# Spreading the value and sum matmuls of the first batch over the units, and reordering the second pair, in a hash-attention and maxout-FFN kernel

## The chip, the cores and the metric

The kernel runs on one core of a Trainium2 chip. Its engines work side by side and meet through semaphores: TensorE (PE, with weight loads listed as PEld), VectorE (DVE), ScalarE (ACT), GpSimd (POOL), and SyncE (SP), which here only issues DMAs. The metric is device time in microseconds of one execution; the time of the kernel before is the median of three.

## The reference

```python
def _attn_ref(q, k, v, proj):                      # q, k, v: 4 x 8 x 768 x 64, proj: 64 x 6
    scale = 1.0 / np.sqrt(D)
    q_bits = (np.einsum('bhsd,dk->bhsk', q, proj) > 0).astype(np.int64)
    k_bits = (np.einsum('bhsd,dk->bhsk', k, proj) > 0).astype(np.int64)
    q_bucket = np.sum(q_bits * powers, axis=-1)
    k_bucket = np.sum(k_bits * powers, axis=-1)
    mask = q_bucket[:, :, :, None] == k_bucket[:, :, None, :]
    scores = scale * np.matmul(q, k.transpose(0, 1, 3, 2))
    scores = np.where(mask, scores, -1000000000.0)
    ...                                            # softmax over keys
    return np.matmul(attn, v)

def _moe_ref(x, w1, w2, w3, w_out):                # x: 3072 x 512 from the heads, w1..w3: 512 x 768
    h = np.maximum(np.maximum(x @ w1, x @ w2), x @ w3)
    return h @ w_out                               # w_out: 768 x 512
```

Queries and keys of a head are hashed to six bits; a query attends only to keys in its bucket. The heads of a token, side by side, are the input of a three-way maxout layer and an output projection.

## The kernel before, in words

**Pairs and units.** Two heads make a pair; there are 16 pairs, four to a batch. A pair is computed in 12 units, six for each half of the queries (qh, 384 queries). One unit is one head (hd) and two of the six chunks of 128 keys (kp). So there are 192 units; a group is six units with the same pair and query half, and slot is the unit's number within it. For each unit `scores` (L299 on) does two matmuls of bf16 operands from the tile S into a two-bank PSUM tile sc (pool of two), and ACT takes the exponential into one of 14 fp16 tiles AT. S holds for each side (0 queries, 1 keys) and head 64 rows of data and six rows of bits (plus or minus 0.5), in an even and an odd half of the positions, so that a matmul over 70 rows gives the score with the bucket penalty.

**Preparation of a pair** (`prep_groups`). Four transpose groups (`tgroup`: three PE transposes into a PSUM tile mp, a DVE copy to the SBUF tile T2, and for pairs 2 to 7 a second DVE copy of the odd rows to S). The first of them runs `begin`, which also issues on POOL the q and k loads of the pair two further on. Then `hashes`: eight matmuls of T2 with the projection into bp, the comparison on DVE (bits, L208), and four DMAs that put bits into S (L214), on POOL's queue, though for pair 1 those of head 0 go by SP. Then `even`, one POOL cast (L217), and for pair 1 `odd`, two DVE casts (L221). `do_hash` calls the odd casts given as the last list, then the hash, and appends the rest to the list `late`, from which one entry is taken in each unit. For pair 1 that list is odd, odd, even.

**Values and sums.** With the exponentials of six units there, 24 matmuls of 32 columns give the values (av, one PSUM bank in a pool of its own) and 12 give partial sums (sm, from the pool ms_ps of three banks, which transposes, hashes and the FFN use too). DVE then empties them: sv (L350), avs (L351), ys (L353). In `values` they run one unit behind the group. From the second pair to unit 59 the value matmuls of the first four chunks run at slot 4 of the group itself (`EARLY_CH`). The sums pass through DMAs (dd, rd, rb) for the normalisation: gather, then `invert`, `spread` and `scale` at set numbers of units later; scale, on POOL, writes xT, the FFN's input (L388).

**The order** is written out by hand in one loop over the units (L415 on). In unit u it issues: loads of v and of weights due there, `scores(u + 1)`, normalisation steps that are due, one entry of `late`, then on some slots a transpose group or a hash (`fill`), the early values, FFN groups once the batch is complete (from unit 61 on), and after a group's end the values. Every engine executes its own instructions in this order. Ahead of the loop stand nine warming matmuls (L400) and the first pair's preparation. After unit 60 two query halves are evaluated together, and the change leaves that part alone.

**Unit order within a group.** For pair 0 the units are sorted by head (head 0's three units, then head 1's); for the others head alternates.

Of the kernel before, what the change touches and what calls it, by code (L numbers as in the profile page):

```python
# [9 lines left out]
FP32 = mybir.dt.float32  # L10
# [7 lines left out]
def kernel(  # L18
# [12 lines left out]
    nc = tc.nc  # L31
    B, H, S, D = q.shape
    NBITS = proj.shape[1]
    P = 128
    NCH = S // P

    HALF = S // 2
    CH2 = NCH // 2
# [17 lines left out]
    ODD_LATE, ODD_PSUM = 1, 8  # L56
# [18 lines left out]
    av_ps = ctx.enter_context(tc.tile_pool(name="av_ps", bufs=1, space=bass.MemoryType.PSUM))  # L75
    ms_ps = ctx.enter_context(tc.tile_pool(name="ms_ps", bufs=3, space=bass.MemoryType.PSUM))
# [9 lines left out]
    def load_proj():  # L86
        for par in range(2):
            rows = slice(par * D, (par + 1) * D)
            nc.scalar.dma_start(pst[rows, :], proj[:, :])
            nc.vector.tensor_copy(pj[rows, 1 + par, 0:NBITS], pst[rows, :])  # L90
            nc.vector.tensor_copy(pj[rows, 0, par : 2 * NBITS : 2], pst[rows, :])
# [3 lines left out]
    ones = konst.tile([P, 32], FP16, name="ones")  # L95
    nc.vector.memset(ones[:], 1.0)

    NAT = 14
    at_tiles = [konst.tile([P, 2, HALF + 2], FP16, name=f"AT{i}", tag=f"AT{i}") for i in range(NAT)]
# [7 lines left out]
    natural, trans, vones = {}, {}, {}  # L107
# [25 lines left out]
    def prep_groups(pi):  # L133
# [85 lines left out]
        def odd(side):  # L219
            copy = nc.scalar.copy if pi > ODD_LATE else nc.vector.tensor_copy  # L220
            return lambda: copy(st["S"][0:D, side, :, 1, :], st["T2"][D : 2 * D, side])  # L221
# [7 lines left out]
                    lambda: bits_first(1, early[2:]), lambda: bits_first(0, ((0, 1, 0, HALF),)),  # L229
                    lambda: bits_first(1, ((0, 1, 0, HALF),))]  # L230
        odds = [odd(1), odd(0)]
        if pi == ODD_LATE:
            return [tgroup(s, h) for h in (0, 1) for s in (1, 0)], hashes, odds + [even], []
        return [tgroup(s, h) for h in (0, 1) for s in (1, 0)], hashes, [even], odds if pi >= ODD_PSUM else []

    def ffn_groups(b):
        xb = xts[b]
# [44 lines left out]
    units = []  # L282
    for pi in range(NPAIR):
        for qh in range(2):
            inner = [(kp, hd) for kp in range(NCH // 2) for hd in range(2)]
            units += [(pi, qh, kp, hd) for kp, hd in (sorted(inner, key=lambda e: e[1]) if pi == 0 else inner)]
    unit_of = {e: u for u, e in enumerate(units)}
    NU = len(units)
    UPB = NU // B
    UPG = NCH  # L290
    UPP = 2 * UPG
    WEIGHTS_AT = (2, 4, 6, 8) + tuple(range(12, 48, 5)) + (63, 67, 71)
    FFN_AT = 13
    EARLY_CH = 4
    FIRST = 2
    PAIRS_AT = UPB + UPP
    xts, avs_of, ys_of = {}, {}, {}
# [18 lines left out]

    started = {}

    def values_part(pi, qh, c0, c1, own=True):
        if (pi, qh) not in started:  # L320
            started[pi, qh] = (av_ps if own else ms_ps).tile([P, 512], FP32, tag="av" if own else "ms", name="av")
        av = started[pi, qh]
        for c in range(c0, c1):
            for hd in range(2):
                at = at_tiles[unit_of[pi, qh, c // 2, hd] % NAT]
                for vh in range(2):
                    p0, d0 = hd * D + 32 * vh, c * D + 32 * vh
                    nc.tensor.matmul(av[p0 : p0 + 32, 0 : HALF + 1], vones[pi][:, hd, d0 : d0 + 32],  # L328
                                     at[:, c % 2, 0 : HALF + 1], start=(c == 0), stop=(c == NCH - 1))
        return av  # L330

    def values(pi, qhs, c0=0):
        at_of = lambda qh, hd, c: at_tiles[unit_of[pi, qh, c // 2, hd] % NAT]
        banks = []
        for qh in qhs:
            av = values_part(pi, qh, c0, NCH, qh == qhs[0])
            sm = ms_ps.tile([P, 512], FP32, tag="ms", name="sm")
            for s in range(CH2):
                for hd in range(2):
                    for half in range(2):  # L340
                        c, t = half * CH2 + s, 2 * hd + half
                        nc.tensor.matmul(sm[32 * t : 32 * t + 32, 0:HALF], ones[:, :],  # L342
                                         at_of(qh, hd, c)[:, c % 2, 0:HALF], start=(s == 0), stop=(s == CH2 - 1))
            banks.append((qh, av, sm))
        if pi not in avs_of:
            avs_of[pi] = avspool.tile([P, 2, HALF], FP32, tag="avs", name="avs")
            ys_of[pi] = yspool.tile([P, 2, HALF], FP32, tag="ys", name="ys")
        for qh, av, sm in banks:
            sv = small.tile([P, 1], FP32, tag="sv", name="sv")
            nc.vector.tensor_scalar(out=sv[:], in0=av[:, HALF : HALF + 1], scalar1=EPS, scalar2=None, op0=AluOp.mult)  # L350
            nc.vector.tensor_scalar(out=avs_of[pi][:, qh, :], in0=av[:, 0:HALF], scalar1=sv[:], scalar2=None,  # L351
                                    op0=AluOp.add)
            nc.vector.tensor_scalar(out=ys_of[pi][:, qh, :], in0=sm[:, 0:HALF], scalar1=EPS * S / 2, scalar2=None,  # L353
                                    op0=AluOp.add)
        if pi % HPAIR == HPAIR - 1:
            return normalize(pi, qhs[0], 1)
        return normalize(pi, 0, 2) if 1 in qhs else []
# [38 lines left out]

    with tc.manual_schedule():
        wm = ms_ps.tile([P, 512], FP32, tag="ms", name="wm")
        for _ in range(9):
            nc.tensor.matmul(wm[:], warm[:, 0:P], warm[:], start=True, stop=True)  # L400
        load(0, nc.sync)
        load_proj()
        load(1, nc.sync)
        cast_v = {0: load_v(0, nc.sync)}
        load(2, nc.sync)
        first = prep_groups(0)
        for g in first:
            g()

        prep, hash_ready, late, ffn, steps = [], [], [], [], []  # L410
        f_credit = 0.0
        for p2 in range(1, NPAIR):
            ts, *hs = prep_groups(p2)
            prep += [(p2, i, g, hs) for i, g in enumerate(ts)]
        for u in range(NU):  # L415
            pi = units[u][0]
            b, ub = divmod(u, UPB)
            if u % UPP == 0 and pi + 1 < NPAIR:
                cast_v[pi + 1] = load_v(pi + 1, nc.gpsimd)
            if u == FIRST:  # L420
                cast_v[0]()
            if u % UPP == 10 and pi + 1 < NPAIR:
                cast_v[pi + 1]()
            if u in WEIGHTS_AT:
                nc.gpsimd.dma_start(*weight_parts.pop(0))
            if ub == FFN_AT and b > 0:
                ffn += ffn_groups(b - 1)
            if FIRST < u + 1 < NU:
                scores(u + 1)
            for e in [e for e in steps if e[0] <= u]:  # L430
                e[1]()
                steps.remove(e)
            if late:
                late.pop(0)()
            slot = u % UPG
            if u <= UPG:
                fill = u >= FIRST
            else:
                fill = slot in (2, 3, 5) if u < UPB + FFN_AT else slot in (1, 4)
            if fill:  # L440
                if hash_ready and u < PAIRS_AT:
                    do_hash()
                elif prep and prep[0][0] < pi + AHEAD:
                    _, i, g, hs = prep.pop(0)
                    g()
                    if i == 3:
                        hash_ready.append(hs)
            if slot == 4 and UPP < u < PAIRS_AT:
                values_part(*units[u][0:2], 0, EARLY_CH)
            f_credit = min(f_credit + 0.66, 1.4)  # L450
            while ffn and f_credit > 0:
                c, g, _ = ffn.pop(0)
                g()
                f_credit -= c
            if u >= UPG - 1 + LAG and (u - LAG) % UPG == UPG - 1:
                vp, vq = units[u - LAG][0:2]
                single = vp * UPP < PAIRS_AT or vp % HPAIR == HPAIR - 1
                if single or vq == 1:
                    steps += [(u + n, g) for n, g in values(vp, (vq,) if single else (0, 1),
                                                            EARLY_CH if (vp, vq) in started else 0)]  # L460
                    if u >= PAIRS_AT and vq == 1:
                        do_hash()

        steps = [(n - NU, g) for n, g in steps]
        steps += values(NPAIR - 1, (1,))
        steps.sort(key=lambda e: e[0])
        at = 0
        for c, g, _ in ffn + ffn_groups(B - 1):
            while steps and steps[0][0] <= at:
                steps.pop(0)[1]()  # L470
            g()
            at += c
# [30 lines left out]
```

## Time and profile before

| what | value |
|---|---|
| median of three executions | 299.92 us (297.75 to 301.09) |
| profiled execution, its own time | 300.85 us |
| its span, first to last instruction | 299.1 us |
| mean granted TensorE clock | 0.988 |
| PE busy | 288.8 us (97%) |
| ACT busy | 194.6 us (65%) |
| DVE busy | 190.3 us (64%) |
| POOL busy | 139.8 us (47%) |
| DMA moved | 35.90 MB |

The span is shorter than the time by what lies around the first and last instruction. Busy times are of one execution, each engine by itself; they overlap. The slices of the page are 40 equal parts of the span, each about 7.5 us, with a digit for tenths of busy time. A unit of the first batch takes about 0.95 us (seven groups from 34.26 to 74.55 us); the FFN's first matmul starts at 75.21 us.

### The profile page before, as it was taken

The numbers are of one execution on the slowest core, as the hardware profiler recorded it, in microseconds if no ns is written. First come the engines' busy times: TensorE is split into PE (matmuls) and PEld (weight loads), VectorE is DVE, ScalarE is ACT, GpSimd is POOL, SyncE is SP. The second block draws the span as 40 slices with busy tenths as digits, with TensorE's granted clock in tenths as the row PEclk, the third lists the DMA queues.
The fourth block names the chain that finished last, engine by engine and source line by source line (L and its number), as shares of the span: only waits on it lengthen the run. The fifth ranks groups of instructions, "written<-read, shape, count | busy, mean of one in ns | idle before, by whom it ended". The sixth has DMA issues, their size and how long they took to land.

```text
span 299.1 us, 6790 instructions
## 1 busy us (share of the span) xinstructions
PE 288.8 (97%) x2593; PEld 162.6 (54%) x2593; DVE 190.3 (64%) x419; ACT 194.6 (65%) x238; POOL 139.8 (47%) x187
## 2 busy tenths in 40 slices
PE   8879999899999999999999999999999999999994
PEld 3444444444566556565566556665655555555551
DVE  2873688877877367663777467663766266758480
ACT  3764888988584966879586966879596957110202
POOL 2762769888874718184723808082700702220000
PEclk9995999999999999999999999999999999999999
DMA  7885088767593442618050452414111211230202
GB/s 211 263 196 154 13 235 184 152 191 212 138 256 104 147 142 66 209 33 278 20 161 30 124 177 59 109 33 160 33 56 37 96 51 46 80 132 2 105 0 106
DMA packets 20277, 35.90 MB, mean 120 GB/s; under 512 B 6081, under 2 KB 12485, under 8 KB 20245
## 3 DMA queue, kind: packets, MB, share of 16 engines
q0 software_dynamic: 8992, 19.81, 24.9%
q1 hardware_dynamic: 10948, 15.52, 16.7%
q8 instruction: 20, 0.33, 0.5%
q10 hardware_dynamic: 304, 0.13, 0.2%
q14 instruction: 13, 0.10, 0.1%
HBM read 31.46 MB, written 6.39 MB: 127 GB/s over the span
## 4 chain that ended last, share of the span: by engine, by line
PE 90%; DMA 3%; ACT 2%; POOL 2%; DVE 1%; issue 1%; SPq 0%; ACTq 0%; POOLq 0%
PE l L246 31%; PE sc L304 21%; PE av L328 11%; PE l L262 10%; PE mp L150 6%; PE sm L342 5%; PE bp L205 4%; DMA rb<-rd 2%; ACT AT L307 2%; PE wm L400 1%; PE bp L191 1%; DMA rd<-rr 1%; POOL S L217 1%; POOL S L214 0%; POOL xT L388 0%
## 5 line engine op out<-in xcount | busy, mean ns | idle before, releaser
L307 ACT ACTIVATE AT<-sc,bias_t 128x768 f16<-128x768 f32 x192 | 168.1, 904 | 59.8 <-PE sc L304 55.1
L246 PE MATMUL l<-xT,w_sb 128*128 128x384 f16 x576 | 110.2, 326 | 0.1
L304 PE MATMUL sc<-S 70*128 70x384 bf16 x384 | 93.7, 330 | 5.1 <-ACT AT L307 3.0
L246 PEld LDWEIGHTS <-w_sb 128*128 128x128 f16 x576 | 55.8, 97 | 35.6 <-issue 0.6
L214 POOL DMA_DIRECT2D S<-bits x58 | 32.9, 570 | 88.3 <-DVE bits L208 58.2
L253 DVE TENSOR_TENSOR ht<-ht,l 128x384 f16<-128x384 f16 x96 | 53.0, 552 | 19.3 <-PE l L246 14.3
L304 PEld LDWEIGHTS <-S 70*128 70x128 bf16 x384 | 34.6, 98 | 45.9 <-issue 21.4
L388 POOL TENSOR_TENSOR xT<-avs,rb 128x384 f16<-128x384 f32 x32 | 31.5, 999 | 34.0 <-DMA rb<-rd 29.4
L251 DVE CAST ht<-l 128x384 f16<-128x384 f32 x48 | 26.6, 553 | 26.2 <-PE l L246 25.0
L328 PE MATMUL av<-AT,vo 128*32 128x385 f16 x768 | 40.1, 335 | 0.0
L262 PE MATMUL l<-wout_sb,ht 128*128 128x512 f16 x144 | 36.5, 379 | 0.0
L276 ACT COPY osb<-l 128x512 f32<-128x512 f32 x23 | 13.5, 585 | 35.0 <-PE l L262 28.4
L328 PEld LDWEIGHTS <-vo 128*32 128x32 f16 x768 | 18.4, 97 | 17.8 <-issue 10.9
L160 DVE COPY T<-mp 128x384 f32<-128x384 f32 x31 | 17.0, 549 | 16.5 <-PE mp L150 13.7
L158 DVE TENSOR_SCALAR T<-mp 128x384 f32<-128x384 f32 x30 | 16.6, 552 | 14.0 <-PE mp L150 12.6
L217 POOL CAST S<-T 64x1536 bf16<-64x1536 f32 x15 | 22.2, 1477 | 0.0
L342 PE MATMUL sm<-AT,ones 128*32 128x384 f16 x384 | 21.9, 331 | 0.0
L262 PEld LDWEIGHTS <-ht 128*128 128x128 f16 x144 | 14.0, 97 | 12.7
L351 DVE TENSOR_SCALAR avs<-av,sv 128x384 f32<-128x384 f32 x32 | 19.8, 618 | 1.6
L353 DVE TENSOR_SCALAR ys<-sm 128x384 f32<-128x384 f32 x32 | 17.5, 548 | 0.1
L150 PE MATMUL mp<-iden,knat 128*128 128x128 f32 x96 | 16.3, 279 | 0.0
L150 PE MATMUL mp<-iden,qnat 128*128 128x128 f32 x96 | 16.0, 275 | 0.0
(45 smaller groups left out, 182.6 us busy)
## 6 DMA issues: line engine op xcount, KB each, us to landing
out_dram<-osb SPq DMA_DIRECT2D x23, 256.0 KB
vnat<-in_v_dram POOLq DMA_DIRECT2D x15, 384.0 KB, 4.9
knat<-in_k_dram POOLq DMA_DIRECT2D x13, 384.0 KB, 4.4
qnat<-in_q_dram POOLq DMA_DIRECT2D x13, 384.0 KB, 5.1
rb<-rd SPq DMA_DIRECT2D x24, 192.0 KB
w_sb<-in_moe_w_dram POOLq DMA_DIRECT2D x12, 192.0 KB, 4.4
rb<-rd SPq DMA_DIRECT2D x16, 96.0 KB
S<-bits POOLq DMA_DIRECT2D x58, 9.0 KB, 2.3
```

What stands on the lines that cost most here:

```text
L150: nc.tensor.transpose(mp[:, i * P : (i + 1) * P], n[:, hd, 2 * i * D : (2 * i + 2) * D], iden[:])
L214: eng.dma_start(st["S"][D:KR, side, hd, :, :], bits[p0 : p0 + 2 * NBITS, :])
L217: nc.gpsimd.tensor_copy(st["S"][0:D, :, :, 0, :], st["T2"][0:D])
L246: nc.tensor.matmul(ps[:, 0:HALF], w_sb[wi][:, jc, fb * P : (fb + 1) * P], xb[:, jc, hf * HALF : (hf + 1) * HALF], start=(jc == 0), stop=(j ...
L251: nc.vector.tensor_copy(hts[fb][:], ps[:, 0:HALF])
L253: nc.vector.tensor_tensor(out=hts[fb][:], in0=hts[fb][:], in1=ps[:, 0:HALF], op=AluOp.max)
L262: nc.tensor.matmul(st2["l2"][:, 0:DM], hts[fb][:, tb * P : (tb + 1) * P], wout_sb[:, fb, :], start=(fb == 0), stop=(fb == NFB - 1))
L304: nc.tensor.matmul(sc[:, j, 0:HALF], th[0:KR, 1, hd, j, kp * P : (kp + 1) * P], th[0:KR, 0, hd, qh, :], start=True, stop=True)
L307: nc.scalar.activation(at[:, :, 0:HALF], sc[:, :, 0:HALF], ActFn.Exp, bias=bias_t[:], scale=SCALE)
L328: nc.tensor.matmul(av[p0 : p0 + 32, 0 : HALF + 1], vones[pi][:, hd, d0 : d0 + 32], at[:, c % 2, 0 : HALF + 1], start=(c == 0), stop=(c == ...
L342: nc.tensor.matmul(sm[32 * t : 32 * t + 32, 0:HALF], ones[:, :], at_of(qh, hd, c)[:, c % 2, 0:HALF], start=(s == 0), stop=(s == CH2 - 1))
L388: return lambda: nc.gpsimd.tensor_mul(xt[:, jj, (q0 + i) * HALF : (q0 + i + 1) * HALF], avs[:, q0 + i, :], rb[:, i, :])
```

## The change

Six edits, all in the head of the program and in the first batch:

1. The warming matmuls are eight instead of nine.
2. Pair 1's odd casts are called by `do_hash` ahead of the hash, and its `late` list holds only the even cast.
3. Units are sorted by head for the first query half of pairs 0 and 1 (before: both halves of pair 0).
4. `values_part` now does values and sums together, for two of the six chunks at a time. At slot 2 it runs for units 0 and 1 of the group, at slot 4 for units 2 and 3, and the last third runs with the group's end, at slot 0 of the next. The sums' bank is taken with the first part. The halves of chunks that make up the four partial sums change from low and high to even and odd chunks; their number stays.
5. These parts run for every group from unit 8 to unit 59 but for the first half of pair 1 (units 12 to 17), whose values and sums run whole at unit 18.
6. Transposes and hashes of the units from 7 on come at slots 1, 3 and 5 instead of 2, 3 and 5.

```diff
-        if pi == ODD_LATE:
-            return [tgroup(s, h) for h in (0, 1) for s in (1, 0)], hashes, odds + [even], []
-        return [tgroup(s, h) for h in (0, 1) for s in (1, 0)], hashes, [even], odds if pi >= ODD_PSUM else []
+        return [tgroup(s, h) for h in (0, 1) for s in (1, 0)], hashes, [even], odds if pi == ODD_LATE or pi >= ODD_PSUM else []
...
-            units += [(pi, qh, kp, hd) for kp, hd in (sorted(inner, key=lambda e: e[1]) if pi == 0 else inner)]
+            units += [(pi, qh, kp, hd) for kp, hd in (sorted(inner, key=lambda e: e[1]) if pi <= ODD_LATE and qh == 0 else inner)]
...
-    def values_part(pi, qh, c0, c1, own=True):
+    def values_part(pi, qh, s0, s1, own=True):
         if (pi, qh) not in started:
-            started[pi, qh] = (av_ps if own else ms_ps).tile([P, 512], FP32, tag="av" if own else "ms", name="av")
-        av = started[pi, qh]
-        for c in range(c0, c1):
+            av = (av_ps if own else ms_ps).tile([P, 512], FP32, tag="av" if own else "ms", name="av")
+            started[pi, qh] = av, ms_ps.tile([P, 512], FP32, tag="ms", name="sm")
+        av, sm = started[pi, qh]
+        for s in range(s0, s1):
+            ats = [at_tiles[unit_of[pi, qh, s, hd] % NAT] for hd in range(2)]
+            for c in (2 * s, 2 * s + 1):
+                for hd in range(2):
+                    for vh in range(2):
+                        p0, d0 = hd * D + 32 * vh, c * D + 32 * vh
+                        nc.tensor.matmul(av[p0 : p0 + 32, 0 : HALF + 1], vones[pi][:, hd, d0 : d0 + 32],
+                                         ats[hd][:, c % 2, 0 : HALF + 1], start=(c == 0), stop=(c == NCH - 1))
             for hd in range(2):
...
+                for half in range(2):
+                    t = 2 * hd + half
+                    nc.tensor.matmul(sm[32 * t : 32 * t + 32, 0:HALF], ones[:, :], ats[hd][:, half, 0:HALF],
+                                     start=(s == 0), stop=(s == CH2 - 1))
+        return av, sm
+
+    def values(pi, qhs, s0=0):
+        banks = [(qh, *values_part(pi, qh, s0, CH2, qh == qhs[0])) for qh in qhs]
...
-        for _ in range(9):
+        for _ in range(8):
...
-                fill = slot in (2, 3, 5) if u < UPB + FFN_AT else slot in (1, 4)
+                fill = slot in (1, 3, 5) if u < UPB + FFN_AT else slot in (1, 4)
...
-            if slot == 4 and UPP < u < PAIRS_AT:
-                values_part(*units[u][0:2], 0, EARLY_CH)
+            if slot in (2, 4) and UPG < u < PAIRS_AT and u // UPG != 2:
+                values_part(*units[u][0:2], slot // 2 - 1, slot // 2)
...
-                                                            EARLY_CH if (vp, vq) in started else 0)]
+                                                            CH2 - 1 if (vp, vq) in started else 0)]
```

More of the change, by code (lines that the diff above doesn't have):

```diff
@@ L293 @@
     FFN_AT = 13
-    EARLY_CH = 4
     FIRST = 2
@@ L317 @@
     started = {}
-    def values_part(pi, qh, c0, c1, own=True):
+    def values_part(pi, qh, s0, s1, own=True):
         if (pi, qh) not in started:
-            started[pi, qh] = (av_ps if own else ms_ps).tile([P, 512], FP32, tag="av" if own else "ms", name="av")
-        av = started[pi, qh]
-        for c in range(c0, c1):
-            for hd in range(2):
[L325 to L344, printed above, removed]
+            av = (av_ps if own else ms_ps).tile([P, 512], FP32, tag="av" if own else "ms", name="av")
```

## The prediction

> **What bounds the kernel now.** I read the page first, then the busy time by windows, then the chain of waits in the stretches where TensorE (PE) is not full, then the timeline there. From the page:
>
> ```profile
> span 299.1 us, 6790 instructions
> ...
> PE 288.8 (97%) x2593; PEld 162.6 (54%) x2593; DVE 190.3 (64%) x419; ACT 194.6 (65%) x238; POOL 139.8 (47%) x187
> ...
> PE   8879999899999999999999999999999999999994
> ...
> PEclk9995999999999999999999999999999999999999
> ```
>
> PE is busy for 97% of the span, and its idle time lies in the first slices. From about 75 us the digits are nines to the end, and the change touches only units up to 59. So whatever is won before 75 us moves the end by as much, and nothing can be won behind it. Slice 4 (22 to 30 us) has a second loss, at PEclk 5. The windows (length, busy time of PE, PEld, DVE, ACT, POOL, clock, DMA) measure both:
>
> ```profile
> 9.00:12.40 3.40, 2.70 (x16) 0.88 (x16) 2.38 (x8) 2.60 (x3) 3.40 (x6) 1.00 0.87 292
> ...
> 19.30:22.70 3.40, 1.36 (x8) 0.73 (x8) 2.82 (x6) 2.56 (x4) 3.40 (x5) 0.97 0.71 155
> 22.70:26.10 3.40, 3.40 (x27) 1.78 (x31) 1.11 (x2) 1.80 (x2) 1.84 (x3) 0.50 0.82 231
> 26.10:29.50 3.40, 3.40 (x31) 1.66 (x20) 1.34 (x3) 0.91 (x2) 0.00 (x0) 0.53 0.39 83
> ```
>
> From 19.3 to 22.7 us PE works 1.36 of 3.40 us, and for the next 6.8 us its clock is half. POOL is full in the same window. The chain of waits says with what:
>
> ```profile
> 16.69 0.57 DVE bits L208
> ...
> 17.54 1.08 POOL S L214 x2
> ...
> 18.70 0.50 POOL w_sb L425
> ...
> 19.62 0.75 POOL knat L115
> ...
> 21.06 1.51 POOL S L217
> ...
> 24.72 2.05 PE av L328 x24
> ```
>
> and the timeline says who waits, and what ACT, DVE and SP do meanwhile:
>
> ```profile
> 17.28 1.79 SPq L214 DMA_DIRECT2D S<-bits  x2
> ...
> 18.58 3.28 ACT L307 ACTIVATE AT<-sc,bias_t 128x768 f16<-128x768 f32 x4 [1.93 <-PE sc L304]
> ...
> 18.95 1.03 DVE L221 CAST S<-T 64x768 bf16<-64x768 f32 x2
> ...
> 22.62 0.82 PE L304 MATMUL sc<-S 70*128 70x384 bf16 x2 [1.81 <-POOL S L217]
> ```
>
> The scores of unit 12 (first of the second pair) wait 1.81 us for the even half of S, which POOL casts at 21.06, behind two bits DMAs, a weight DMA and the q and k loads that pair 2's first transpose group issues.
>
> **The change part by part.** *Second pair reordered.* The even cast now comes out of the late list at unit 7 instead of 9, right behind the two bits DMAs (17.54 plus 1.08, so about 18.7) and ahead of the weight DMA and the loads. It ends near 18.7 + 1.5 = 20.2, not 22.57. The odd casts (1.03 us on DVE) move ahead of the bits; the hash matmuls run on PE meanwhile, so the bits come only about 0.1 later, and the DMAs on SP and POOL with them. The SP pair then is issued by 19.2. When it lands no row shows, but the bounds are: not before 19.2, and not over 3.5 us behind its issue, since unit 12 started at 22.62 with the issue over at 19.07. I take 2, so 21.1. The weight DMA and the loads go out behind the cast, the loads some 1.5 us later than they do, for a pair that is transposed 20 units on.
>
> By head at first: units 12 to 17 take head 0 first, whose bits go by SP; values of these six units therefore come whole at unit 18. Nothing is added. In the first pair the second query half loses that order, so its values can start at unit 8.
>
> What is late next? Values parts at units 8 and 10 (0.6 us each, below) and a transpose at 7 instead of 8 fill PE before unit 12. My walk: scores 8 at 18.04, PE reaches scores 12 at about 21.5, S is there at 21.1 (22.7 at worst, which would cost 1.2). ACT has its exps 8 to 11 done at 18.58 + 3.28 = 21.86, so exp 12 starts near 22.1 instead of 23.48. From there ACT sets the pace: 3.28/4 = 0.82 a unit, six exps to 27.0, plus 0.3 where the hash at unit 15 holds PE. Scores 19 then go at 27.4 and the nine rounds of values (1.6 us) end at 29.4. Before, that place is 34.26. **Head: 4.8 us.** It checks against the two losses: 1.81 of wait, and at most half of the 6.8 us at half clock, 3.4, of which I count 3.1 since ACT would have held PE for a part; together 4.9. If the clock still falls, 3.1 of it is lost again.
>
> At this place a rule speaks against the cure being needed. The Trainium skill, "TensorE: Matmul & The Clock Gate" (Why this matters for your kernels), asks for no PE gaps over about 3 us. This trace differs: the clock fell after a wait of 1.81 us, in a window 40% busy, so I go by the window's share. By the rule alone the wait would be the only gain, 1.8.
>
> *Values and sums in three parts.* The rows of one group of six units at full clock:
>
> ```profile
> 37.02 0.84 PE L328 MATMUL av<-AT,vo 128*32 128x385 f16 x16
> ...
> 37.79 0.50 PE L304 MATMUL sc<-S 70*128 70x384 bf16 x2
> ...
> 38.12 0.49 PE L150 MATMUL mp<-iden,qnat 128*128 128x128 f32 x3
> 38.45 0.49 PE L304 MATMUL sc<-S 70*128 70x384 bf16 x2
> 38.87 0.51 PE L328 MATMUL av<-AT,vo 128*32 128x385 f16 x8
> 39.22 0.66 PE L342 MATMUL sm<-AT,ones 128*32 128x384 f16 x12
> 39.81 0.82 PE L304 MATMUL sc<-S 70*128 70x384 bf16 x4
> 40.56 0.85 PE L205 MATMUL bp<-T,pj 128*32 128x384 f32 x8
> ...
> 46.91 0.48 PE L304 MATMUL sc<-S 70*128 70x384 bf16 x2 [0.40 <-ACT AT L307]
> ```
>
> Start to start, a pair of scores costs 0.33, or 0.42 ahead of values; three transposes 0.33; a hash 0.80. Sixteen value matmuls take 0.77 (four rounds of four), eight and twelve sums 0.94 (five rounds): 0.165 a round and 0.12 to leave the shape. Now it is three times three rounds, 3 × 0.615 = 1.85 instead of 1.71, and one more 0.42: about 0.2 more a group. Against it stands ACT: with two scores back to back (39.81) and then only a transpose, PE runs ahead and waits 0.40 as at 46.91. Spread over units 0, 2 and 4, with fills at 1, 3 and 5, two units cost PE 0.70 + 1.02 against ACT's 1.64, so that wait goes, and no hash follows its last transpose by one unit any more. From unit 18 to 48 the window says
>
> ```profile
> 34.26:63.45 29.19, 27.61 (x305) 13.58 (x301) 23.07 (x49) 25.07 (x31) 24.23 (x33) 1.00 0.76 181
> 63.45:75.92 12.47, 12.02 (x131) 6.29 (x128) 10.54 (x26) 10.99 (x14) 11.60 (x17) 1.00 0.63 167
> ```
>
> By the prices, a new group takes 3 × 0.42 + 3 × 0.33 + 1.85 = 4.1 for scores and values; five of them, with 12 transpose groups and 3 hashes (0.80, and 0.09 for the scores ahead), take 20.5 + 4.0 + 2.7 = 27.2, a gain of 2.0 at most. But there is a new wait: the single av bank must be emptied before unit 2 rather than unit 4.
>
> ```profile
> 40.20 0.62 DVE L351 TENSOR_SCALAR avs<-av,sv 128x384 f32<-128x384 f32 x1
> 40.73 0.55 DVE L353 TENSOR_SCALAR ys<-sm 128x384 f32<-128x384 f32 x1
> ```
>
> Here avs ended 1.0 us behind the end of the sums at 39.81, with DVE busy on transposes before it. PE now needs the bank 0.33 + 0.33 + 0.42 = 1.08 behind its last part: anything from no wait to 0.5 a group (DVE is 23.07 of 29.19 busy). Behind that wait stand the next scores and with them ACT. So the groups give between +2.0 and, if DVE is late every time, −0.5. **I take 1.0**, the middle towards the av row.
>
> *Nine warming matmuls become eight.*
>
> ```profile
> 1.19 4.02 PE L400 MATMUL wm<-warm 128*128 128x512 f16 x9 [1.19 <-DVE warm L79]
> ...
> 4.58 0.23 PEld L150 LDWEIGHTS mp<-iden,knat 128*128 128x128 f32 x1 [0.28 <-issue]
> ...
> 5.01 0.70 PE L150 MATMUL mp<-iden,knat 128*128 128x128 f32 x3
> ```
>
> The first transposes wait for PE's own queue, not for data, so up to 0.43 (4.02/9 less the overlap) is free; 0 if the second k load sets the pace, or if the first transposes run slow for longer. **I take 0.3.**
>
> *Units 48 to the FFN: nothing.* The FFN's fourth matmul waits for the last quarter of xT:
>
> ```profile
> 66.10 1.75 DMA rd<-rr
> ...
> 68.41 6.31 DMA rb<-rd
> ...
> 74.88 1.00 POOL xT L388
> ...
> 75.92 0.99 PE l L246 x5
> ```
>
> That chain hangs on the sums of unit 48 and takes 12.47 us from 63.45 whatever PE does. PE has nearly that much work there, so 0 to 0.4 that the groups would win is swallowed. All that is won before 63.45 shifts the chain too and is kept.
>
> **Sum.** The profiled execution took 300.85 (span 299.1 and 1.75 around it): 300.85 − 4.8 − 1.0 − 0.3 = **294.75, say 294.8**. The three runs shown have a median of 299.92 and lie between 297.75 and 301.09, so the profiled one is 0.9 above; I do not take that off, since a run that happened to lose less clock would also win less. Its own range: head 3.6 to 4.9, groups −0.5 to 2.0, warming 0 to 0.43: 293.5 to 297.8.
>
> **Rivals.**
>
> *The clock falls all the same.* Units 13 to 17 have no values and are paced by ACT; I count 2.45 us of PE work in 3.3 there, 74%. It fell at 40% (19.30) and not at 79% (9.00). If 74% is too little, or the bits land as late as 22.7 and PE idles again, 3.1 comes back: 297.9. Chance 0.12.
>
> *A bank wait makes it slower.* The sums' bank is now held from unit 2 to the next unit 0, one of three that the transposes and hashes use. If the transposes at unit 1 are given that bank in turn, they wait for L353. From the rows at 39.81 and 40.73 it is empty 1.5 us behind the last part (40.73 + 0.55 − 39.81); PE is there after one pair of scores, 0.33. That is some 1.2 to 1.4 in seven groups (units 13, 25 to 55), 9.4. Against it: the slot-3 bank is free far earlier, and a pool that gives out the one free first never does this. It decides from 0.9 a group on; at 1.35, 300.85 − 5.1 + 9.4 = 305.2. Chance 0.08.
>
> *Given back at the FFN.* The rd<-rr hop took 1.75 here, but for pair 2 the spread could start only long after:
>
> ```profile
> 57.65 0.31 SPq L380 DMA_DIRECT2D rd<-rr  x1
> ...
> 63.41 1.16 SPq L384 DMA_DIRECT2D rb<-rd  x2
> ```
>
> That is 5.8 us, beside loads and weights. Where pair 3's hop meets loads in the same way, xT is up to 3.7 later: 298.5. For it: POOL and DMA are busy there. Against: the loads move with the same units. Chance 0.07.
>
> *Slow start.* If the clock rises only once PE has worked long enough, one matmul less may miss the moment. At most it would cost what the later drop cost, 3.4; that early PE waits for DVE and ACT too, so I take half and some, 1.8: 296.6. No drop shows here with nine. Chance 0.07. The Trainium skill, "TensorE: Matmul & The Clock Gate" (Part 4), says that transposes do not count towards the full clock, and transposes are what follows the warming; no run here shows it yet.
>
> **How the numbers follow.** The forecast has 0.66. A measurement of this kernel tells about 1% from no change, 3 us around 299.92, so faster means below 296.9. The forecast gives 0.64 of its 0.66 there, the slow start and the milder clock drops 0.06 more: 0.70. The clock, the FFN and the upper end of the forecast make 0.22 within 1%. The bank makes 0.08 slower. The range reaches from the forecast's low end to the two cases near 298: 293.2 to 298.6; it leaves out the bank wait and the corners.
>
> **What would show it.** Right: the scores of unit 12 with a wait under 0.3, the even cast starting before 19.5 us, clock 1.00 in every window from 19 to 30, the values of unit 18 ending near 29; no 0.40 waits of scores for ACT from 30 to 58; the FFN starting near 69.5 us. Wrong: a clock of 0.5 anywhere, transposes waiting for L353, av waiting over 0.5 for L351, or FFN waiting over 1.5 us for rb<-rd.

## The result, and the profile after

| | before | changed |
|---|---|---|
| median of six executions, us | 300.17 (297.75 to 301.16) | 295.92 (295.49 to 296.50) |
| profiled execution, us | 300.85 | 295.93 |
| its span, us | 299.1 | 294.0 |
| mean granted clock | 0.988 | 0.998 |

The ratio is 0.9874 with a 95% interval of 0.9827 to 0.9921: faster by 1.3%, about 4 us. The forecast was faster by over 1%, 294.8 us in a range of 293.2 to 298.6. From the page of the changed kernel:

```profile
span 294.0 us, 6792 instructions
...
PE 285.0 (97%) x2592; PEld 159.7 (54%) x2592; DVE 188.7 (64%) x419; ACT 195.4 (66%) x238; POOL 139.7 (48%) x187
...
PE   8898999998999999999999999999999999999994
...
PEclk9999999999999999999999999999999999999999
```

PE is busy 3.8 us less, although its work is the same but for one warming matmul. Most of the difference is the clock: the 5 in the fourth slice is gone, and 6.8 us at half clock are 3.4 us more of busy time. The same windows as before the change (length, busy times of PE, PEld, DVE, ACT, POOL, clock, DMA):

```profile
19.30:22.70 3.40, 3.32 (x42) 1.74 (x38) 2.37 (x5) 3.26 (x5) 3.40 (x5) 1.00 0.36 95
22.70:26.10 3.40, 3.00 (x30) 1.31 (x29) 3.09 (x7) 3.33 (x5) 1.47 (x3) 1.00 0.94 276
26.10:29.50 3.40, 3.00 (x48) 1.72 (x45) 1.68 (x3) 2.71 (x4) 2.38 (x5) 1.00 0.49 111
```

PE works 3.32 of 3.40 us where it worked 1.36, and the clock stays at 1.00. The timeline of POOL and PE shows the reordered second pair:

```profile
17.52 1.17 POOL L214 DMA_DIRECT2D S<-bits  x2 [3.31 <-DVE bits L208]
18.68 1.48 POOL L217 CAST S<-T 64x1536 bf16<-64x1536 f32 x1
20.09 0.75 POOL L115 DMA_DIRECT2D knat<-in_k_dram  x1
...
21.56 0.48 PE L301 MATMUL sc<-S 70*128 70x384 bf16 x2
...
29.70 0.50 PE L301 MATMUL sc<-S 70*128 70x384 bf16 x2
```

The even cast begins at 18.68 instead of 21.06, ahead of the loads; the scores of unit 12 (21.56) wait for nothing that shows; the values of unit 18 end at 29.70, where they ended at 34.26. Now the two stretches behind (units 18 to 48, and from there to the FFN's fourth matmul), and the waits in them:

```profile
29.70:57.68 27.98, 27.26 (x304) 12.63 (x301) 22.18 (x48) 25.16 (x30) 24.79 (x34) 1.00 0.75 189
57.68:71.05 13.37, 12.10 (x131) 5.98 (x128) 11.44 (x27) 11.76 (x14) 12.28 (x17) 1.00 0.58 155
```

```profile
53.13 0.51 PE L327 MATMUL av<-AT,vo 128*32 128x385 f16 x8 [0.68 <-DVE avs L344]
...
59.13 0.51 PE L327 MATMUL av<-AT,vo 128*32 128x385 f16 x8 [0.30 <-POOL vo L125]
...
71.05 1.62 PE L244 MATMUL l<-xT,w_sb 128*128 128x384 f16 x9 [0.97 <-POOL xT L381]
```

The four waits of 0.40 us of scores for ACT in this stretch are gone; one av wait for avs (0.68) and one for the v cast (0.30) have come. The five groups take 27.98 us instead of 29.19. But the last stretch is longer, 13.37 instead of 12.47, and ends in a wait of 0.97 us. The chain into it:

```profile
60.65 1.36 DMA rd<-rr
...
62.59 7.28 DMA rb<-rd
...
70.01 1.00 POOL xT L381
...
71.05 1.62 PE l L244 x9
```

So the profiled executions differ by 4.56 us in the head, plus 1.21 in the groups, minus 0.90 ahead of the FFN; some 0.2 more come behind it. That is the 5.1 us between the spans.

The order of POOL's work ahead of the FFN has changed too. In the kernel before, xT stands ahead of pair 6's even cast:

```profile
74.88 1.00 POOL L388 TENSOR_TENSOR xT<-avs,rb 128x384 f16<-128x384 f32 x1 [0.87 <-DMA rb<-rd]
75.81 1.46 POOL L217 CAST S<-T 64x1536 bf16<-64x1536 f32 x1
```

and in the changed kernel behind it:

```profile
68.33 1.48 POOL L217 CAST S<-T 64x1536 bf16<-64x1536 f32 x1
70.01 0.99 POOL L381 TENSOR_TENSOR xT<-avs,rb 128x384 f16<-128x384 f32 x1 [0.21 <-DMA rb<-rd]
```

This comes from the sixth edit. With slots 1, 3 and 5 pair 6 is hashed in unit 55 instead of 56, so its even cast leaves the list `late` in unit 56; this xT is issued in unit 57.

**What the spread of the kernel before hides.** In the first set of experiments below the kernel before ran 25 times. Five executions had a clock of 0.997 or 0.998 and took 297.54 to 298.39 us; twenty had 0.994 or less and took 299.78 to 301.33. Half clock for 3.4 us takes 0.006 off the mean, for 6.8 us 0.011; E11's profile has 0.997 from the last 1.7 us of its span alone. So those five show no fall in the head, and the price of the fall is over 2 us. The changed kernel's 14 executions in three measurements all had 0.998 or more.

### The profile page after: what moved, and what is told of

Read it like the earlier page. It is cut to its first block, busy times and chain, and to the rows that moved or that the text cites. A ratio compares the mean times of both kernels' runs of the same rounds, so it can differ in the third digit from the quotient of the medians.

```text
span 294.0 us, 6792 instructions
## 1 busy us (share of the span) xinstructions
PE 285.0 (97%) x2592; PEld 159.7 (54%) x2592; DVE 188.7 (64%) x419; ACT 195.4 (66%) x238; POOL 139.7 (48%) x187
## 4 chain that ended last, share of the span: by engine, by line
PE 90%; DMA 3%; DVE 2%; ACT 2%; issue 1%; POOL 0%; SPq 0%; ACTq 0%; POOLq 0%; DVEq 0%
PE l L244 32%; PE sc L301 21%; PE av L327 11%; PE l L260 11%; PE mp L150 6%; PE sm L332 5%; PE bp L205 3%; DMA rb<-rd 2%; ACT AT L304 2%; PE wm L393 1%; PE bp L191 1%; DMA rd<-rr 0%; DVE S L168 0%; POOL xT L381 0%; DVE rr L372 0%
## 5 line engine op out<-in xcount | busy, mean ns | idle before, releaser
L301 PEld LDWEIGHTS <-S 70*128 70x128 bf16 x384 | 33.8, 98 | 41.7 <-issue 20.2
L327 PE MATMUL av<-AT,vo 128*32 128x385 f16 x768 | 48.3, 330 | 1.0 <-DVE avs L344 0.7
L332 PE MATMUL sm<-AT,ones 128*32 128x384 f16 x384 | 32.7, 324 | 0.0
L327 PEld LDWEIGHTS <-vo 128*32 128x32 f16 x768 | 17.3, 95 | 20.0 <-issue 10.9
L346 DVE TENSOR_SCALAR ys<-sm 128x384 f32<-128x384 f32 x32 | 17.5, 548 | 0.0
L343 DVE TENSOR_SCALAR sv<-av 128x1 f32<-128x1 f32 x32 | 5.1, 158 | 18.3 <-PE av L327 17.8
```

What stands on the lines that cost most here:

```text
L301: nc.tensor.matmul(sc[:, j, 0:HALF], th[0:KR, 1, hd, j, kp * P : (kp + 1) * P], th[0:KR, 0, hd, qh, :], start=True, stop=True)
```

## The experiments

Each kernel stands beside runs of the kernel before on the same chip. The medians of that kernel were 300.19 (E1 to E4), 300.79 (E5 to E8) and 300.46 (E9 to E12).

### E1 and E2: each half of the change alone

E1 is the kernel before with the list edit only:

```diff
-        if pi == ODD_LATE:
-            return [...], hashes, odds + [even], []
-        return [...], hashes, [even], odds if pi >= ODD_PSUM else []
+        return [...], hashes, [even], odds if pi == ODD_LATE or pi >= ODD_PSUM else []
```

> The kernel before with only the second pair reordered (odd casts ahead of the hash, even cast at unit 7). My theory: the 1.81 us wait of the scores of unit 12 for the even cast goes, and the clock stays at 1.00 from 19 to 30 us, so this edit alone gives most of the head: 3.5 to 4.8 us, the sum of the values' end of unit 18 near 29.5 to 31. Rival: without values at units 8 and 10 PE still works too little in that window (about 55 to 65% of 3.4 us) and the clock falls all the same; then only 1 to 2 us are won. Second rival: the spreading of the values made the gain and this edit alone gives under 1 us.

E2 is the changed kernel with that edit undone.

> The changed kernel with the second pair's old order (hash, bits, then odd, odd, even at units 7, 8, 9). My theory: the scores of unit 12 wait for the even cast again, until about 22.6 us, but the values at units 8 and 10 fill about 1.2 us of that, so the wait is 0.7 to 1.2 us and PE works some 70% of the window; if the clock follows the busy share, it stays at 1.00 and the kernel loses about 1 us against the changed one. Rival: any wait of about 1 us here brings the clock down, then it loses 3 to 4 us and is about as slow as the kernel before.

E1: 296.88 us (296.24 to 299.51), ratio 0.9909 (0.9876 to 0.9941). E2: 297.85 us (297.13 to 298.61), ratio 0.993 (0.9906 to 0.9955). The reordering alone wins 3.3 us, the parts alone 2.3, both together 4.3: they share one gain, since each by itself holds the clock where it fell. For E2 the window and the wait read

```profile
19.30:22.70 3.40, 2.63 (x34) 1.13 (x31) 3.36 (x5) 3.10 (x4) 3.40 (x5) 1.00 0.68 210
```

```profile
22.71 0.50 PE L303 MATMUL sc<-S 70*128 70x384 bf16 x2 [0.77 <-POOL S L217]
```

The even cast is as late as ever, but the values at units 8 and 10 fill PE, the wait is 0.77 instead of 1.81, PE is 77% busy, and the clock is 1.00. That is as expected, though the kernel loses nearer 2 us than 1 against the changed one. It also waits longer for xT ahead of the FFN, 1.2 us where the changed kernel waits 0.97 (us in total, times, longest):

```profile
PE l L246 <- POOL xT L383: 1.2, 1, 1.2
```

E1 brought something that I had not expected. Eight of its ten executions had a clock of 0.999 or 1.0 and took 296.24 to 297.23 us; two, the profiled one among them, had 0.994 and took 299.44 and 299.51. In the profile the clock falls earlier:

```profile
10.00:13.40 3.40, 2.07 (x12) 0.48 (x9) 3.31 (x6) 2.41 (x3) 3.40 (x6) 1.00 0.67 201
...
13.60:17.00 3.40, 3.40 (x16) 2.63 (x15) 2.50 (x6) 2.39 (x3) 1.37 (x3) 0.54 1.00 240
```

```profile
13.41 0.48 PE L302 MATMUL sc<-S 70*128 70x384 bf16 x2 [1.33 <-DVE S L196]
```

Here the first scores started late (9.29 us, against 8.58), PE then waited 1.33 us for the first pair's bits in a window that is 61% busy, and was at half clock for the next 3.4. Where the other one fell is not known. The kernel before and the changed one have the same code at this place.

### E3: PE kept busy while it waits

```diff
+            if u == 2 * UPG - 1:
+                wk = ms_ps.tile([P, 512], FP32, tag="ms", name="wk")
+                for _ in range(8):
+                    nc.tensor.matmul(wk[:], warm[:, 0:P], warm[:], start=True, stop=True)
             if FIRST < u + 1 < NU:
                 scores(u + 1)
```

> The kernel before with eight matmuls of zeros (128x512, about 1.7 us, read by nobody) put on PE ahead of the scores of unit 12, where PE is idle. The even cast is as late as before. If the clock fell because PE idled, it now stays at 1.00 and the kernel is about 3 us faster than before although the scores still start near 22.6; if the clock falls for another reason (or zeros do not count as work), nothing is won, and the window from 22.7 to 29.5 shows about 0.5 again.

298.54 us (297.51 to 299.35), ratio 0.995 (0.9922 to 0.9978), all ten clocks 0.997 or more. The windows:

```profile
19.30:22.70 3.40, 3.06 (x19) 1.60 (x17) 3.31 (x7) 3.01 (x4) 3.40 (x5) 1.00 0.74 162
22.70:26.10 3.40, 3.40 (x49) 2.02 (x48) 2.40 (x6) 1.70 (x3) 1.94 (x3) 1.00 0.77 245
```

Useless work on zeros holds the clock at 1.00, with the even cast as late as before: without PE's idleness there is no fall. It is worth 1.65 us of the median, less than the 3 I expected. The reference explains little of that: without the five executions that kept their clock its median would be 300.27 instead of 300.19. In the profiles the values of unit 18 end 2.8 us earlier (31.47 against 34.26) and the FFN's fourth matmul only 2.1 (73.83 against 75.92): this kernel waits 0.8 us for xT there. E1, which takes the wait itself away as well, is 1.7 us faster than E3.

### E4, E7 and E9: the wait ahead of the FFN

E4 issues pair 8's loads, which stand ahead of the rb<-rd transfer, later:

```diff
-            if 2 < pi + 2 < NPAIR:
+            if 2 < pi + 2 < NPAIR and pi != 6:
                 load(pi + 2, nc.gpsimd)
...
+            if u == 61:
+                load(8, nc.gpsimd)
```

> The changed kernel with the q and k loads of pair 8 (768 KB) issued at unit 61 instead of unit 47. In the changed kernel they are issued on POOL at 61.01 and 61.74 us, just ahead of the rb<-rd transfer on which the FFN's first matmul group waits (7.28 us, against 6.31 in the kernel before). If the loads are what lengthens it, rb<-rd takes 5 us or less, the FFN's wait of 0.97 us goes, and the kernel is 0.8 to 1.0 us faster than the changed one. Rival: the transfer's time is its own many small packets; then it stays near 7 us and nothing is won.

296.54 us (295.82 to 297.03), ratio 0.9882 (0.9844 to 0.992), against 0.9874 of the changed kernel, which was not run beside it: nothing won. The FFN still waits 0.7 us, now for POOL's own order. Its timeline:

```profile
66.37 2.30 POOL L214 DMA_DIRECT2D S<-bits  x4 [2.29 <-DVE bits L208]
68.67 1.48 POOL L217 CAST S<-T 64x1536 bf16<-64x1536 f32 x1
70.11 1.00 POOL L381 TENSOR_TENSOR xT<-avs,rb 128x384 f16<-128x384 f32 x1
```

The multiplication that makes xT stands behind the bits DMAs and the even cast of pair 6 and starts as they end, without a wait for the transfer. The loads did lengthen the transfer: its 128 packets, the pieces in which it is moved, end at 66.34 us here and at 69.33 in the changed kernel, after issues at 62.09 and 62.03. So the first half of my theory holds and the rival fails, but nothing is won, since the even cast holds xT as long. E7 adds an earlier chain:

```diff
-[(7, invert), (11, spread), (15, scale(0))]
+[(6, invert), (10, spread), (13, scale(0))]
```

> The changed kernel with pair 8's loads at unit 61 and, for the single query halves, invert, spread and scale at 6, 10 and 13 units instead of 7, 11 and 15. In the kernel with the later loads alone the last quarter of xT was no longer held by the transfer but by POOL's own order: the bits DMAs and the even cast of pair 6 (66.37 to 70.15 us) stood ahead of it. With scale ahead of them the FFN's wait of 0.97 us should go and the kernel be 0.7 to 1.0 us faster than the changed one (about 295.0). Rival: the wait at this place is made good behind it anyway; then the FFN starts sooner but the time stays.

297.09 us (296.60 to 298.12), ratio 0.987 (0.9831 to 0.9908), some 0.8 slower than the changed kernel beside it (296.25). The transfer now takes 4.66 us:

```profile
61.89 4.66 DMA rb<-rd
```

The FFN waits no more for xT, but two others wait:

```profile
59.77 0.51 PE L327 MATMUL av<-AT,vo 128*32 128x385 f16 x8 [0.95 <-DVE avs L344]
...
79.25 0.52 PE L150 MATMUL mp<-iden,knat 128*128 128x128 f32 x3 [0.69 <-DMA knat<-in_k_dram]
```

The earlier invert holds DVE ahead of avs, and so the av bank; and pair 8's loads, behind everything else on POOL, now come too late. E9 mends both: loads at unit 56, invert at 7, spread at 11, scale at 13.

> The changed kernel with pair 8's loads at unit 56 (not 47, and not 61 as before, where its transposes then waited 0.69 us for them) and scale at 13 units instead of 15, ahead of pair 6's bits DMAs; invert and spread as in the changed kernel, since an earlier invert held avs on DVE and av on PE for 0.95 us. My theory: the FFN's wait of 0.7 to 1.0 us goes and nothing new is waited for: 0.5 to 1.0 us faster than the changed kernel, 295.3 to 295.7. Rival: the bits and the even cast of pair 6, now behind scale, or the loads, are waited for in their turn, and the time stays within 0.3 us.

295.59 us (295.01 to 296.68), ratio 0.9844 (0.9821 to 0.9867); the changed kernel beside it (E12) had 295.76 and 0.9843 (0.9822 to 0.9865). No difference can be told, so this is the rival's case. The wait for xT is gone, and behind it stand two smaller ones, of FFN matmuls for a PSUM bank that DVE is late to empty:

```profile
69.81 0.81 PE L244 MATMUL l<-xT,w_sb 128*128 128x384 f16 x4 [0.18 <-DVE ys L346]
70.85 0.82 PE L244 MATMUL l<-xT,w_sb 128*128 128x384 f16 x4 [0.23 <-DVE S L168]
```

From the FFN's first matmul to its last block of twenty (critical chain) E9 takes 250.70 − 68.81 = 181.89 us. The changed kernel takes 251.66 − 69.43 = 182.23 with the 0.97 wait in it. So of 0.97 only 0.34 is won: the wait stood in front of DVE's backlog, which would have held PE for most of it.

### E5, E6, E10 and E12: the warming matmuls and the start

E5 and E12 are the changed kernel again.

> The changed kernel itself, beside the three that follow: 295.5 to 296.5 us by its first measurement (295.92). Its profile shows again whether the clock stays at 1.00 from 19 to 30 us, and how far the first scores' start (8.56 us in its first profile) moves from execution to execution: in the four runs so far it lay between 8.76 and 9.29. Expected between 8.5 and 9.3; a rival that the start is fixed by the program would give 8.56 again.

> The changed kernel again, for the three beside it: 295.5 to 297.1 us as in its two measurements so far, clock 0.998 or more in every run. If the clock's fall in the head can still happen with this order of work, one of the runs shows 0.994 or less and a time near 299.

E5: 296.25 us (295.93 to 297.09), ratio 0.9841 (0.9795 to 0.9888). E12: 295.76 (295.45 to 296.44), as above. The first scores start at 8.95 and 8.10 us, 8.56 in the first profile, so the start moves by 0.9 us for one and the same program, further than I had bounded it. No run of either shows a fall of the clock. E12 shows a wait for the bits that SP issues:

```profile
21.34 0.48 PE L301 MATMUL sc<-S 70*128 70x384 bf16 x2 [0.33 <-DMA S<-bits]
```

E6 and E10 put the ninth warming matmul back, E6 in the changed kernel and E10 in E9.

```diff
-        for _ in range(8):
+        for _ in range(9):
```

> The changed kernel with nine warming matmuls. I had given the ninth's removal 0.3 us; the profile of the changed kernel shows the first transposes starting 0.43 us earlier but running slower until about 5.9 us, and the first scores at 8.56 against 8.58. My theory now: the clock is let go by time, not by the number of matmuls, so the ninth costs nothing: within 0.2 us of the changed kernel. Rival, the prediction's: 0.3 us slower than the changed one. Rival the other way: the ninth keeps PE at work and the start is steadier, up to 0.3 us faster.

> The kernel with scale first and later loads, with nine warming matmuls. Nine gave 295.83 against 296.25 with eight (four runs each), within their spread. If the ninth makes the start steadier, this is 0.2 to 0.5 us faster than the same with eight; if the start's time is chance, the two agree within 0.3 us.

E6: 295.83 us (295.27 to 296.44), ratio 0.9824 (0.9777 to 0.987), against 296.25 with eight. E10: 295.53 (295.08 to 296.18), ratio 0.9828 (0.9809 to 0.9847), against 295.59. Within 0.4 and 0.1 us, with ranges that overlap: the ninth matmul makes no difference that these runs can tell, and the prediction's 0.3 us are not seen. PE's timeline says why. The changed kernel:

```profile
1.19 3.59 PE L393 MATMUL wm<-warm 128*128 128x512 f16 x8 [1.19 <-DVE warm L79]
4.58 0.85 PE L150 MATMUL mp<-iden,knat 128*128 128x128 f32 x3
5.22 0.85 PE L150 MATMUL mp<-iden,qnat 128*128 128x128 f32 x3
...
8.56 0.48 PE L301 MATMUL sc<-S 70*128 70x384 bf16 x2 [0.26 <-DVE S L196]
```

and E6, with one more:

```profile
1.19 3.49 PE L393 MATMUL wm<-warm 128*128 128x512 f16 x9 [1.19 <-DVE warm L79]
4.52 0.49 PE L150 MATMUL mp<-iden,knat 128*128 128x128 f32 x3
...
8.19 0.48 PE L301 MATMUL sc<-S 70*128 70x384 bf16 x2 [0.27 <-DVE S L196]
```

Three transposes take 0.85 us while the clock is low and 0.49 when it is up. In E6 it is up from 4.00 us, nine matmuls taking 3.49 where they took 4.02; in the changed kernel only from 5.96; in E1, also with nine, from 7.02. The moment differs by up to 3 us between executions, and it moves the start more than the count does. Where the moment is nearly the same, profiles with nine start later than those with eight: 9.29 (E1, clock up at 7.02) against 9.02 (E2, 6.98), 8.19 (E6, 4.00) against 7.86 (E9, 4.03) and 8.22 (E10, 4.70) against 8.10 (E12, 4.75).

In E10's profile the bits come later still:

```profile
22.19 0.49 PE L301 MATMUL sc<-S 70*128 70x384 bf16 x2 [1.05 <-DMA S<-bits]
```

PE waits 1.05 us, and the clock holds.

### E8: the old slots

```diff
-                fill = slot in (1, 3, 5) if u < UPB + FFN_AT else slot in (1, 4)
+                fill = slot in (2, 3, 5) if u < UPB + FFN_AT else slot in (1, 4)
```

> The changed kernel with transposes and hashes at slots 2, 3 and 5 again. Slot 2 then holds scores, transposes and a values part (1.4 us of PE against 0.82 of ACT), slot 1 only scores: PE waits for ACT ahead of it and ACT starves behind it. By my prices 0.1 to 0.4 us a group is lost: 0.5 to 2.5 us slower than the changed kernel. Rival: the parts alone smooth enough and the slots do not matter: within 0.3 us.

296.91 us (296.41 to 302.00), ratio 0.9851 (0.9805 to 0.9897). Five of the six executions lie between 296.41 and 297.61, with a median of 296.66 against 296.25: 0.4 us slower, between the two theories and inside the spread, so the slots' price stays open. The profiled execution is the sixth, which took 302.0 us because its clock fell, and it shows how:

```profile
61.23 0.51 PE L327 MATMUL av<-AT,vo 128*32 128x385 f16 x8 [1.29 <-POOL vo L125]
```

```profile
59.00:62.00 3.00, 1.59 (x18) 0.83 (x18) 2.48 (x7) 1.77 (x3) 3.00 (x5) 0.95 0.51 148
62.00:65.00 3.00, 3.00 (x19) 1.26 (x18) 1.12 (x2) 1.80 (x2) 3.00 (x5) 0.50 0.46 62
```

One wait of 1.29 us for the v cast, in a window 53% busy, and the clock is 0.50 until 71.96 us. The changed kernel has the same wait, at 59.13, of 0.30. Here xT stands ahead of pair 6's even cast again, and the FFN does not wait for it; with the clock down just before, that does not price the order.

### E11: heads alternate in the second pair

```diff
-sorted(inner, key=lambda e: e[1]) if pi <= ODD_LATE and qh == 0 else inner
+sorted(inner, key=lambda e: e[1]) if pi < ODD_LATE and qh == 0 else inner
...
-            if slot in (2, 4) and UPG < u < PAIRS_AT and u // UPG != 2:
+            if slot in (2, 4) and UPG < u < PAIRS_AT:
```

> The changed kernel without the head order in the second pair: units 12 to 17 alternate heads and their values run in parts at units 14, 16 and 18. By my walk the bits of both heads are there when unit 12 starts, and from 12 to 17 ACT sets the pace, so values put there cost nothing and the whole block at unit 18 (1.6 us of PE, with ACT idle) shrinks to one part: 0.5 to 1.0 us faster than the changed kernel. Rival: head 1's bits, issued by POOL at 18.1 us, land only after 22.2 us; then the scores of unit 13 wait and it is up to 1 us slower.

296.30 us (295.74 to 296.55), ratio 0.9856 (0.9835 to 0.9876): 0.5 above E12 beside it, with ranges that overlap, and not faster. The walk was right as far as it went: the scores that follow the values of unit 18 start at 29.02 instead of 29.70, and unit 13 does not wait. Then it is given back:

```profile
30.71 0.51 PE L327 MATMUL av<-AT,vo 128*32 128x385 f16 x8 [0.53 <-DVE avs L344]
...
59.84 0.51 PE L327 MATMUL av<-AT,vo 128*32 128x385 f16 x8 [1.08 <-POOL vo L125]
```

PE runs into the av bank 0.53 us earlier than DVE empties it, and into the v cast, whose place in POOL's queue has not moved. In this kernel the head order is no gain of its own, but neither does undoing it help.

## Why the prediction was right, point by point

**What bounds the kernel: right.** The wait for the even cast and the fall of the clock behind it were most of the gain. E1 takes away the wait, E2 fills it with values, E3 with zeros; in all three profiles the clock stays up at that place.

**Head, 4.8 us: right, measured 4.56.** The walk gave 29.4 for the end of unit 18's values; it was 29.70. The even cast starts at 18.68 (predicted 18.7). Unit 12's scores start at 21.56 (predicted 21.5). The bound on the bits' landing was needed: E12 and E10 wait for them, 0.33 and 1.05 us; that they cost nothing in the first profile is in part luck.

**Groups, 1.0 us in a range of −0.5 to 2.0: right, measured 1.21.** The 0.40 waits for ACT went, and the av bank took one wait of 0.68 in five groups. An av wait of over 0.5 was on the prediction's list of signs of being wrong; it came once, inside the range given for it. A value part costs what the price said: from 39.81 to the scores behind it at 40.41, 0.60 against 0.615.

**Warming, 0.3 us: not seen.** The step that failed is that the first transposes would run as fast 0.43 us earlier. They start earlier, at 4.58, but at the low clock, 0.85 for three, and the first scores start at 8.56 against 8.58. The lower bound, 0, named this. In part it was luck of the moment: the clock came up at 5.41 us in the profile before and at 5.96 in this one. Where the moments agree, profiles with eight do start 0.1 to 0.3 us earlier, too little to see in the times. The rival in which eight matmuls miss the moment is not borne out either: with eight it came at 4.03 in E9. That transposes would not count towards the full clock, which stood beside this rival, the runs speak against. In E8 the clock stayed down after 0.28 to 3.69 us, 73% busy with warming matmuls, and came up at 7.10 after 3.41 us of full work of which over half was transposes. The Trainium skill, "TensorE: Matmul & The Clock Gate" (Part 1), says that the window that lets the clock go is free-running and does not start with the kernel; the starts here, at full clock from 4.00 in E6 to 7.02 us in E1, agree.

**Units 48 to the FFN, nothing: the step that failed.** I took the chain to be 12.47 us whatever PE does. It was 13.37, a loss of 0.90, and two things that I had left out hold xT. One is the transfer: rb<-rd took 7.28 us instead of 6.31. With pair 8's q and k loads out of its way it takes 4.66 (E7), and its packets end 3 us earlier where only these loads are moved (E4), so the loads lengthen it; why it was shorter in the kernel before, which has the same loads, was not tested. The other is POOL's order: the moved slots put the even cast ahead of xT. In the changed kernel's first profile POOL then waits only 0.21 us more for the transfer; in E4, E5 and E12 it starts xT as the cast ends, at 70.11, 70.03 and 69.87, and the FFN waits 0.7 us all the same. So either alone would hold the FFN about as long, and the kernels that move both, E7, E9 and E10, have no wait there. The cast alone was not moved in a kernel that kept its clock. And E9 shows that the price of this wait is mostly nominal: without it, 0.63 of 0.97 us is lost to DVE behind.

**The rivals.** The bank of the sums makes no transpose wait in the first batch: no row of the changed profile shows a wait of transposes for L346. The fall of the clock that stays did not come in 14 executions, but E8 and E1 show that it was a real one: a wait of 1.3 us in a window 53 or 61% busy is enough. Its count of 74% for PE in units 13 to 17 was too low: the windows from 22.70 and 26.10 show 3.00 of 3.40 us, 88%. The FFN case came in small, and in part by another way, the even cast. Two prices do not follow from their rows, though nothing hangs on them: the bank wait gives 1.47 less 0.33, 1.14 a group and not 1.35, and the FFN case 5.76 less 1.76 (SP's hop, issued at 66.10 and 67.86), 4.0 and not 3.7.

**The sum.** 294.8 against 295.92: 0.9 of the 1.1 us is the FFN chain, 0.3 the warming and 0.24 the head; the groups made 0.21 more than I took, and some 0.2 came behind the FFN's start. By median the gain is 4.25 us, less than the 4.92 of the two profiled executions, because the kernel before does not lose its clock to the full in each execution.

## What to carry to other kernels

Read the granted clock beside the busy share, window by window: a stall of 1.3 to 1.8 us cost more by the half clock behind it (over 2 us) than by itself. Anything that fills PE there helps, and matmuls of zeros prove the cause cheaply. And where a kernel is full, price a wait by what stands behind it: the wait ahead of the FFN, taken away in E9, gave back a third of its length.

## What the runs showed of the hardware that was not expected

The clock fell to half after waits of 1.81 (kernel before), 1.33 (E1) and 1.29 us (E8); it held after 1.2 (E2, for xT), 1.08 (E11) and 1.05 us (E10). The Trainium skill, "TensorE: Matmul & The Clock Gate" (Why this matters for your kernels), puts the limit at gaps of about 3 us; here 1.29 us was enough.

The traces also record when the clock changes. In the kernel before it comes up at 5.41 us, falls at 22.48 and is back at 29.31; in E1 at 7.02, 13.84 and 17.26; in E8 at 7.10, 61.72 and 71.96. From coming up to falling these are 5, 2 and 16 steps of 3.41 us, and the falls last 2, 1 and 3 steps. The fall at the very end lies on the same steps in all 14 profiles (the changed kernel: 5.96 and 292.68, 84 steps). So in these executions the clock changes only on a grid of 3.41 us, and the grid starts elsewhere in each: the changed kernel, one and the same program, found its first full clock at 4.75 (E12), 5.96 and 6.86 us (E5). In every profile it comes up at the end of the first window of this grid that is at least 82% busy (E6, 0.59 to 4.00); 73% was not enough (E8, 0.28 to 3.69).

Cut along that grid, the window that ends with a fall is 41% busy in the kernel before (19.06 to 22.48), 61% in E1 (10.43 to 13.84) and 58% in E8 (58.30 to 61.72). The emptiest windows that kept the clock are 65% busy in E2 (71.83 to 75.25), 68% in E11 (57.30 to 60.71) and 72% in E7 (57.40 to 60.81). E10's 1.05 us is cut in two by the grid, into windows 82 and 83% busy. So a limit between 61 and 65% of a window fits all profiles; one between 1.2 and 1.29 us for a single gap fits them too, and these runs do not tell the two apart. If the window's share decides, it is partly chance whether a wait of this length brings the clock down, since it depends on where the grid cuts it. That would explain why five of 25 executions of the kernel before kept their clock; with one profile of that kernel it is not shown.
